# Fused attention and gated FFN on one core: gate and value sums in chunks among the first batch's scores, a new arrangement of units, stores held at block ends

## Chip, cores and metric

One Trainium2 chip, one of its cores. The metric is the device time of one execution in microseconds (us), the median of several runs. The inputs are float32 in HBM; the kernel computes in bf16 with float32 sums.

## What is computed

```python
# q, k, v: (8, 12, 448, 64); w_gate, w_val: (768, 1536); w_out: (1536, 768)
scores = (1 / sqrt(64)) * q @ k.T                 # per batch and head
attn   = maximum(scores, 0) ** 2 / 448
x      = attn @ v                                 # heads side by side: (3584, 768)
out    = (gelu(x @ w_gate) * (x @ w_val)) @ w_out # (3584, 768)
```

## The kernel before

**Tiles.** TensorE works as four 64x64 quadrants. A sum over 128 rows is cut into a lower row half (`PE0`, r = 0) and an upper one (`PE1`, r = 1), each of two column halves; lower steps of one unit run beside upper steps of another. The 448 tokens of a batch are seven chunks of 64, the twelve heads six pairs (`pr`), two pairs are one third `m` of a batch.

**Units.** For each of the 8 batches there are
- transposes `t` (q and k to `qkT`): batches 0 and 1 on TensorE (`add_transposes`, L628; products with `ident`, L646, the copy out of PSUM L650, for the very first L609 and L617), later ones by DMA transposes on SP's queue (`add_dma_transposes`, L466, issue L480) after a regrouping copy (L475);
- 21 score units `s` (`add_scores`, L677): product `sp<-qkT`, relu on ScalarE (L714, `rl`), square on VectorE (L728, `attnT`). A score unit u belongs to third u // 7; each fourth in a third serves both pairs;
- 6 value units `v` (`add_values`, L761): product `ff<-attnT,v`, scaled copy into `xT` (L792);
- gate and value sums (`add_gate_value`, L1023): per block `fc` of 128 columns of the FFN one sum over six steps `dc` (one for each pair of heads) with `wg` and one with `wv`, gelu on ScalarE (L1044), product with the value sum on VectorE (L1049) into `uT`. From batch 1 on a part of the blocks goes in seven products of a Strassen-like scheme (`add_pair`, L911);
- output products in groups of four chunks of tokens (`add_product`, L1160), seven products with sums on VectorE between them, and stores of `osb` to `out` (L1241): four per group on SP's queue; the last two groups' tiles are stored in halves on SP's and ScalarE's queues.

All TensorE products go through the helper `mm` (L365); products on `warm` (L567, L1430) are filler that keeps TensorE busy while nothing else can run.

**Order.** A planner (`run_plan`, L109) places all operations at build time by costs and due times and writes them down engine by engine; the chip then runs each engine's stream in that order. What it is told:
- `START` (L29) lists the units of batch 0 in order, 0.8 us apart on a scale that ends near 0; this part of TensorE's lower order (`PE0`) is fixed. `PLACE5 = -7.0` (L836) puts the last value unit v5, batch 1's first transposes and three lower steps each of gate 0 and value 0 at one place near its end (L1028).
- `LINE` (L12) lists all later units: a single digit is the next gate or value sum of that batch, `2A1` one of the seven products for batch 2, `a1` one of an output group. `SHIFT` (L35) sets the spans over which scores and values of batches 2 to 7 are spread.
- Loads are issued on GpSimd's queue in the order of L1267 to L1291: q, k, v of batch 0, weight chunk 0, q and k of batch 1 for heads 0 to 3, weight chunk 1, q and k for heads 4 to 7, and so on. The tiles of q and k are two in a ring, so a load waits for the transposes of the third that had its tile.
- `Blocks` (L73) counts TensorE's instructions (a weight load and a product each) in blocks of 256. Marks are set 36 instructions ahead of a block's end; a DMA transpose (`gate`, L139) is planned behind such a mark, and its issue waits for the marked product.
- Stores of groups from the ninth on (`HELD = 8`, L1105; `op.hold`, L147) that the planner would start between 110 instructions ahead of a block's end and 4 behind it are moved to that end, and wait for the product there.

Of the kernel before, what the change touches and what calls it, by code (L numbers as in the profile page):

```python
# [12 lines left out]
0 0 0 0 0 0 0 0 0 0 0 0 0 0 0 0 0 0 0 0 0 0 0 0 1 1A1 1 2 1A6 2 2 1 1A7 1A2 1A5 2 a1 2 a2 2A1 1A4 1  # L13
1 1 1A3 1 2 1 2A2 a6 1 2A7 a7 2 1 a5 1 1 2A6 2 2 1 1 1 1 a3 1 1 a4 1 1 b1 b7 c1 b2 b6 2A4 2 c6 b4 b5
c7 c5 2B1 2B6 c4 2B2 c3 b3 2A5 2 c2 2B7 2B4 2B5 2A3 2 3A1 2 3A2 2 2B3 2 2 3A6 3A7 d7 d1 3B1 d2 4C1
3B2 3 3C1 3B7 3 d6 3 e1 d4 3C7 3 3C6 3 3B6 e7 3B4 e6 3A4 3A5 3 3 3 3C2 3 3B5 3 3 d5 3C4 3A3 3C5 d3
4A1 4C2 3B3 3C3 e5 3 4A7 f1 f2 f6 e4 f7 4C7 4 e2 4C6 4A2 e3 g7 4B1 f5 4B6 4 4A6 4B2 g1 4B7 4 g2 4A5
4C5 4A4 4B4 4B5 f4 4D7 4D1 4C4 4 5B1 5 4D6 4D5 4A3 4 g6 4 g5 4C3 4B3 f3 4 5 5B2 4D2 4D4 g3 4D3 5C1
g4 5B6 5B7 5C2 5B5 5A1 4 5A6 5 5C7 5A7 5A2 5 5B4 5D1 h1 5A4 5D6 5D2 h6 5C6 h7 5 5D7 5D5 5A5 6A1 5B3
5 5C5 5C4 5A3 5C3 5D4 6B1 5 5D3 5 6A2 6B2 h4 i1 i2 6B7 6A6 i7 h5 6A7 h2 6D1 6F7 6D7 h3 j1 6D6 6C1  # L20
6D2 i6 j7 6E1 j6 6C7 6C2 6E7 i5 i4 6C6 6B6 6A5 6A4 6E6 6A3 6F1 6B4 6B5 6C5 6D5 6D4 6F6 i3 6B3 6F5
6C4 j5 6D3 6E2 6F2 6E5 6F4 6C3 6F3 6E4 6E3 7E7 j2 7E1 7B1 k1 k7 7E2 7A1 7B2 7B7 k2 7B6 7E6 j4 7C1 k6
7A2 l7 7C7 7C6 7A7 7B4 7C2 l1 7B5 7B3 k5 7A6 7F1 j3 7D1 7E5 7F7 7F2 7A5 k4 7F6 7E4 l6 7D7 7C4 7D2
7F4 7D6 7D5 7D4 7D3 l2 7F5 7A4 7C5 7C3 7E3 7A3 l5 l4 7F3 m1 n1 m7 k3 l3 m2 m6 n6 m5 n7 n4 m3 n5 n2
m4 n3
# [4 lines left out]
t00 s0 s1 t01 s2 s3 s4 s5 t10 s6 s7 v0 s8 t11 v1 s9 s10 s11 t20 s12 s13 v2 s14 t21 s15 v3 s16 s17  # L30
s18 s19 v4 s20
# [3 lines left out]
SHIFT = "-183 -79.5 40.75 1.75 -343.75 -112 43.75 -179.5 27.25 -513.5 -447.25 0.25"  # L35


class Op:


    def __init__(self, engine, cost, emit, deps=(), lag=0.0, prio=0, other=None):
# [8 lines left out]
        self.hold = False  # L50
# [22 lines left out]
class Blocks:  # L73


    def __init__(self, size, first, lead, near=(0, 0)):
# [4 lines left out]
        self.near, self.edge, self.edges = near, size, []  # L81

    def add(self, ins, n=2):
        self.count += n
        if not self.edges or self.edges[-1][1] is not None:
            if self.count + self.near[0] >= self.edge:
                self.edges.append((self.now, None, None))
        elif self.count >= self.edge + self.near[1]:
            self.edges[-1] = self.edges[-1][0], self.now, ins
            self.edge += self.size  # L90
        if self.count + self.lead >= self.next:
            self.marks.append((self.now, ins))
            self.next += self.size

# [14 lines left out]
def run_plan(queues, pools, units, banks, arrivals, together, fill, blocks, span):  # L109
# [9 lines left out]
    def ready(op):  # L119
# [38 lines left out]
    def next_unit(short):  # L158
# [35 lines left out]
        return best  # L194

# [3 lines left out]
    while left:  # L199
# [70 lines left out]
        op.emit()  # L270
        last = max(last, op.end)
        left -= 1
    return last
# [3 lines left out]
def kernel(  # L277
# [37 lines left out]
    GATE_T, BLOCK = 1.2, 7.1  # L315

    NPB = (0, 1, 2, 3, 4, 4, 6, 6)
    ROOM = 4
    RING_V, RING_T, RING_H, RING_R, RING_A, RING_O = 3, 3, 2, 2, 4, 4
# [39 lines left out]
    blocks = Blocks(256, 256 - 192 + 10, 36, (110, 4))  # L359
# [40 lines left out]
    def load_w12(i):  # L400
        cols = slice(i * WCH, (i + 1) * WCH)

        def emit(wt, src):
            return nc.gpsimd.dma_start(
                wt[:, :, :], src[:, cols].rearrange("(c p) f -> p c f", p=128))
        w12_op[i] = [load(4 * d_model * WCH, lambda wt=wt, src=src: emit(wt, src), rate=rate)
                     for (wt, src), rate in zip(((wg[i], moe_w_gate), (wv[i], moe_w_val)),
                                                (250e3 if i == 1 else 400e3, 400e3))]
# [6 lines left out]
    def load_qk(b, i, h0, h1, deps=()):  # L415
# [12 lines left out]
        for c0, c1, rate in (((0, SC, 400e3 if b else (300e3, 226e3, 420e3)[m]),) if b < EARLY  # L428
# [6 lines left out]
    def load_v(b, h0, h1, deps=()):  # L435

        m = h0 // 4
        for i in range(2):
# [7 lines left out]
            op = load(4 * (h1 - h0) * VC * P * D, emit, deps, rate=(4e6 if h0 == 0 else 400e3) if b == 1 else 400e3 if b else 300e3)  # L446
# [19 lines left out]
    def add_dma_transposes(b, m, deps=()):  # L466
# [28 lines left out]
        for op in tr_op[b, m]:  # L495
            op.gate = GATE_T
        qk_used[b, m] = [copy]
# [130 lines left out]
    def add_transposes(at, b, m, rs):  # L628
# [6 lines left out]
        def emit(r):  # L635
            if b == 0:
                t = new_bank(box["k", r], t_op[b, m, r], [128, SC, 2 * P], bf16)
            else:
                if not box:
                    box["S"] = psS[n].tile([128, 2, 1024], bf16, name="sp", tag="S")  # L640
                t = box["S"][:, r, 0:SC * 2 * P].rearrange("d (c x) -> d c x", c=SC)
            box[r] = t
            src = qk16[b, m].rearrange("p h (c d) -> p h c d", d=D)
# [10 lines left out]
        for r in rs:  # L654
# [6 lines left out]
            mine = b == 0 and f"t{m}{r}a" in START.split()  # L661
# [99 lines left out]
    def add_values(at, b, pr):  # L761
# [6 lines left out]
        def emit(i, w):  # L768
            if 0 not in box:
                box[0] = new_bank(box["k"], x_op[b, pr])  # L770
            if (i, w) == (1, VC - 1) or last and (i, w) == (0, 1):
# [42 lines left out]
        if last:  # L814
            ops[1][0].after = ops[0][1]
            for o, p in zip(ops[1], ops[1][1:]):
                p.after = o
            ops[0][2].deps.append(ops[1][3])
            for i in range(2):
                lower.append((at - 0.6, ops[0][i]))  # L820
# [676 lines left out]
```

## Time and profile before

| | us |
|---|---|
| three timed runs | 396.62, 398.0, 400.57 (median 398.0) |
| profiled execution | 396.92 |
| its span, first to last instruction | 394.9 |

The span is what the rows of the profile cover; the profiled execution's own time is 2.0 us longer. The granted TensorE clock in it is 0.998. In the rows, PE is TensorE's products, PEld its weight loads, DVE VectorE, ACT ScalarE, POOL GpSimd, SP SyncE; `ff`, `sp` are tiles in PSUM. "x72" is a count; behind the bar stand busy us and mean ns of one, then idle time of the engine ahead of the group and what ended it. "issue" is time in which an engine waited for nothing that the profile shows.

### The profile page before, as it was taken

To read this page: it belongs to the slowest core of one execution; us is meant where nothing else is said; L and a number is where in the kernel's file an instruction comes from. 1 tells how busy PE (TensorE), PEld (TensorE's weight loads), DVE (VectorE), ACT (ScalarE), POOL (GpSimd) and SP (SyncE) were. 2 spreads that over 40 slices of the span, in tenths; PEclk is the share of its full clock that TensorE was granted. 3 is DMA by queue.
4 is the path that set the end of the run, shared out by engine and by line. 5 is a ranking of instruction groups with operands and counts; after the bars stand their busy time and mean duration, and the time that the engine had idled before them with its cause. 6 is when DMAs were issued, how large, how long until landed. Compare 5 with 4: busy or idle time off the path is not lost.

```text
span 394.9 us, 22904 instructions
## 1 busy us (share of the span) xinstructions
PE 386.3 (98%) x10570; PEld 358.4 (91%) x10573; DVE 309.6 (78%) x522; ACT 258.7 (66%) x401; POOL 97.2 (25%) x156
## 2 busy tenths in 40 slices
PE   7999999999999999999999999999999999999995
PEld 3458889999999999999999999989999999999994
DVE  3885779968797499999797779758988999866772
ACT  5866872357677767787786478765787886535541
POOL 7656523322233323232332123310211000000000
PEclk9999999999999999999999999999999999999999
DMA  8999999988999969887999598880763501121134
GB/s 110 186 199 199 197 209 185 112 103 83 161 148 175 152 85 143 93 132 121 113 148 108 124 122 111 139 83 11 103 105 56 125 6 43 45 45 45 43 85 120
DMA packets 85567, 45.12 MB, mean 114 GB/s; under 512 B 46048, under 2 KB 82400, under 8 KB 85472
## 3 DMA queue, kind: packets, MB, share of 16 engines
q0 software_dynamic: 46944, 24.39, 49.9%
q1 hardware_dynamic: 37888, 18.49, 26.4%
q8 instruction: 82, 1.34, 1.4%
q10 hardware_dynamic: 640, 0.79, 0.6%
q14 instruction: 13, 0.11, 0.1%
HBM read 48.76 MB, written 11.01 MB: 151 GB/s over the span
## 4 chain that ended last, share of the span: by engine, by line
PE 93%; DVE 2%; DMA 2%; POOL 1%; issue 1%; ACT 0%; ACTq 0%; POOLq 0%
PE ff L365 85%; PE sp L365 7%; DMA qk<-in_k_dram 2%; DVE attnT L728 1%; PE sp L646 1%; POOL qk L424 1%; DVE xT L792 0%; PE ff L646 0%; ACTq L1241 0%; ACT osb L1225 0%; ACT rl L714 0%; PE ff L567 0%; DVE osb L1223 0%; DVE qkT L650 0%; POOL ident masks.py:199 0%
## 5 line engine op out<-in xcount | busy, mean ns | idle before, releaser
L714 ACT ACTIVATE rl<-sp 128x896 bf16<-128x896 f32 x168 | 152.1, 919 | 50.4 <-PE sp L365 45.1
L365 PE MATMUL ff<-xT,wg 64*64 64x224 bf16 (+1 forms) x2304 | 183.7, 299 | 0.6 <-issue 0.6
L365 PEld LDWEIGHTS <-wv 64*64 64x64 bf16 x2304 | 127.7, 107 | 4.4
L365 PEld LDWEIGHTS <-wg 64*64 64x64 bf16 x2304 | 123.3, 107 | 5.0 <-issue 0.5
L365 PE MATMUL ff<-xT,wv 64*64 64x448 bf16 x1056 | 120.8, 349 | 0.0
L728 DVE TENSOR_TENSOR attnT<-rl 128x1792 bf16<-128x1792 bf16 (+1 forms) x98 | 92.2, 952 | 6.6 <-ACT rl L714 6.2
L365 PEld LDWEIGHTS <-ws 64*64 64x64 bf16 x1872 | 92.3, 107 | 1.4 <-issue 1.0
L365 PEld LDWEIGHTS <-s 64*64 64x64 bf16 x1344 | 81.6, 107 | 1.8
L365 PE MATMUL ff<-attnT,v 64*64 64x448 bf16 (+1 forms) x768 | 79.7, 326 | 0.7 <-DVE attnT L728 0.6
L365 PE MATMUL ff<-ts,wv 64*64 64x224 bf16 x1248 | 78.7, 256 | 0.0
L365 PE MATMUL ff<-ts,ws 64*64 64x224 bf16 x1248 | 77.6, 256 | 0.0
L365 PE MATMUL sp<-qkT 64*64 64x448 bf16 (+1 forms) x768 | 74.6, 328 | 0.7 <-issue 0.3
L365 PE MATMUL ff<-wo,s 64*64 64x384 bf16 x672 | 63.4, 323 | 0.0
L966 DVE TENSOR_TENSOR part<-ff,part 128x448 f32<-128x448 f32 x78 | 47.5, 622 | 20.1 <-PE ff L365 16.4
L365 PEld LDWEIGHTS <-uT 64*64 64x64 bf16 x1008 | 62.5, 107 | 0.7
L365 PE MATMUL ff<-wt,s 64*64 64x384 bf16 x672 | 61.4, 322 | 0.0
L365 PE MATMUL ff<-wo,uT 64*64 64x384 bf16 x672 | 60.7, 322 | 0.0
L962 ACT COPY part<-ff 128x448 f32<-128x448 f32 x78 | 41.3, 534 | 12.4 <-PE ff L365 11.2
L443 POOL DMA_DIRECT2D v<-in_v_dram x48 | 29.6, 620 | 80.3 <-ACT rl L714 44.3
L365 PEld LDWEIGHTS <-v 64*64 64x64 bf16 x768 | 44.7, 107 | 4.1 <-issue 1.7
L424 POOL DMA_DIRECT2D qk<-in_q_dram x43 | 27.6, 642 | 80.0 <-ACT rl L714 59.5
L1049 DVE TENSOR_TENSOR uT<-gel,ff 128x448 bf16<-128x448 bf16 x44 | 27.3, 620 | 22.4 <-PE ff L365 11.0
(51 smaller groups left out, 423.9 us busy)
## 6 DMA issues: line engine op xcount, KB each, us to landing
out_dram<-osb SPq DMA_DIRECT2D x48, 192.0 KB, 3.3
v<-in_v_dram POOLq DMA_DIRECT2D x48, 128.0 KB, 4.1
wg<-in_moe_w_gate_dram POOLq DMA_DIRECT2D x6, 384.0 KB, 10.4
wv<-in_moe_w_val_dram POOLq DMA_DIRECT2D x6, 384.0 KB, 11.0
wo<-in_moe_w_out_dram POOLq DMA_DIRECT2D x4, 576.0 KB, 14.9
qk<-in_q_dram POOLq DMA_DIRECT2D x18, 128.0 KB, 3.5
qk<-in_k_dram POOLq DMA_DIRECT2D x18, 128.0 KB, 4.3
qk<-in_q_dram POOLq DMA_DIRECT2D x18, 96.0 KB, 3.8
```

What stands on the lines that cost most here:

```text
L365: ins = nc.tensor.matmul(o, lhsT, rhs, start=start, stop=stop, skip_group_check=onto, tile_position=(P * row, P * col))
L424: return nc.gpsimd.dma_start(qk16[b, m][HALF[i], r0:r0 + h1 - h0, cols], src[b, h0:h1].rearrange("h (p c) d -> p h (c d)", c=SC)[:, :, cols])
L443: return nc.gpsimd.dma_start(v16[b, m][HALF[i], h0 % 4:h0 % 4 + h1 - h0, :, :], v[b, h0:h1].rearrange("h (p c) d -> p h c d", c=SC)[:, :, ...
L646: blocks.add(nc.tensor.transpose(t[HALF[j], c, :], src[:, 2 * r + j, c, :], ident[:, :], tile_position=(0, P * j)))
L714: relu.ins = nc.scalar.activation(duo["rl"][:, u % 2, :, :], box[0][:, :, 0:S], AF.Relu).ins
L728: nc.vector.tensor_tensor(a[:, part], duo["rl"][:, part], duo["rl"][:, part], op=ALU.mult)
L962: rd.ins = nc.scalar.copy(st["t", name][:, :], box[0][:, 0:S]).ins
L966: rd.ins = nc.vector.tensor_tensor(t[:, :], box[0][:, 0:S], t[:, :], op=ALU.add).ins
L1049: u_op[b, fc].ins = nc.vector.tensor_tensor(uT[b][:, fc, :], gel.pop((b, fc))[:, :], box[0][:, 0:S], op=ALU.mult).ins
```

## The change

Five things change.
1. `START` can name `g0`, `g1`, `h0` (steps of gate 0, value 0 and gate 1), `T` (batch 1's first transposes), `w` (the first three lower steps of v5), and `S0`, `S1` (batch 1's first scores). Five lower steps of gate 0 and five of value 0 stand among the last score units; the sixth of each follows at the end. For gate 1 the upper half goes first (`turned`), from the place of `h0` on. `t11` and `t20` stand earlier among the scores. v4's copy goes to ScalarE (`v4a`), and so does the copy of the first of batch 1's transposes (`T_ACT`).
2. `LINE` and `SHIFT` hold another arrangement.
3. Both halves of a third's transposes of batch 1 are written in one run.
4. On SP's and GpSimd's queues, instructions are written down through a queue of their own (`held`). A store of any group but the last, which would be written within 110 instructions ahead of a block's end, is written, with all behind it on its queue, when 4 instructions are left, and waits for the product written last. The rule by planned time and `HELD` go.
5. The order of loads: weight chunk 1 behind batch 1's q and k of heads 4 to 7, v of heads 4 to 7 behind weight chunk 3. The planner's rates of loads are others.

```diff
 START = """
-t00 s0 s1 t01 s2 s3 s4 s5 t10 s6 s7 v0 s8 t11 v1 s9 s10 s11 t20 s12 s13 v2 s14 t21 s15 v3 s16 s17
-s18 s19 v4 s20
+t00 s0 s1 t01 s2 s3 s4 s5 t10 s6 t11 s7 v0 s8 v1 s9 s10 t20 s11 s12 s13 v2 s14 t21 s15 s16 g0 v3 g0
+s17 g0 s18 s19 v4a s20 g1 g0 g1 T w g1 g1 v5 h0 S0 S1 g1 g0
 """
-SHIFT = "-183 -79.5 40.75 1.75 -343.75 -112 43.75 -179.5 27.25 -513.5 -447.25 0.25"
+SHIFT = "-162 -50.25 25.5 2.75 -445.25 -51.75 31.25 -216.75 14.5 -671.5 -361 -10.5"
...
 class Blocks:
...
+    def ahead(self, near, before):
+        edge = -(-(before + near[1]) // self.size) * self.size
+        return edge - near[0] <= before and self.count < edge - near[1]
...
 def run_plan(...):
...
-        if op.hold:
-            for begin, end, ins in blocks.edges[-3:]:
-                if t >= begin and (end is None or t < end):
-                    if end is None and not forced:
-                        return None
-                    t, op.mark = end or t, ins
-            return t
...
+    held = {"SP": deque(), "POOL": deque()}
+    def release(whole=False):
+        for waiting in held.values():
+            while waiting:
+                op, count = waiting[0]
+                if not whole and op.near and blocks.ahead(op.near, count):
+                    break
+                waiting.popleft()
+                if op.near and blocks.count > count:
+                    op.mark = blocks.last
+                op.emit()
+                if waiting:
+                    waiting[0] = waiting[0][0], blocks.count
...
-        op.emit()
+        if e in held:
+            held[e].append((op, blocks.count))
+        else:
+            op.emit()
+        release()
...
+    NEAR_STORE, NEAR_QK, NEAR_V, NEAR_T = (110, 4), None, None, None
...
             else:
-                if not box:
-                    box["S"] = psS[n].tile([128, 2, 1024], bf16, name="sp", tag="S")
-                t = box["S"][:, r, 0:SC * 2 * P].rearrange("d (c x) -> d c x", c=SC)
+                if box:
+                    return
+                box["S"] = psS[n].tile([128, 2, 1024], bf16, name="sp", tag="S")
+                for i in rs:
+                    box[i] = box["S"][:, i, 0:SC * 2 * P].rearrange("d (c x) -> d c x", c=SC)
+                    transpose(i)
+                return
...
-            mine = b == 0 and f"t{m}{r}a" in START.split()
+            mine = f"t{m}{r}a" in START.split() if b == 0 else m == 0 and r < T_ACT
...
 def add_gate_value(at, b, fc, g):
-        if (b, fc) == (0, 0):
-            at = [PLACE5 - 0.5 + 0.1 * g] * 3 + [0.01 * g] * 3
+        early = chunks0.get(f"{'gh'[fc]}{g}") if b == 0 and fc < 2 else None
+        turned = bool(early) and fc == 1
+        if early:
+            at = (early + [0.1 * fc + 0.01 * g] * KC)[:KC]
...
+        if turned:
+            ops[0][0].deps.append(ops[1][-1])
+            for n, op in enumerate(ops[1]):
+                if n:
+                    op.after = ops[1][n - 1]
+                op.prio = 1
+                pairs.append(("from", early[0], [op]))
+            for n, op in enumerate(ops[0]):
+                lower.append((0.1 * fc + 0.01 * g, op))
+        else:
+            then(at, GS, *ops, box, lambda: done)
...
-            op.hold = gr >= HELD
+            op.near = NEAR_STORE if gr < B * SC // 4 - 1 else None
...
     load_qk(1, 0, 0, 4)
     load_qk(1, 1, 0, 4)
-    load_w12(1)
     load_qk(1, 0, 4, 8)
     load_qk(1, 1, 4, 8)
+    load_w12(1)
     load_v(1, 0, 4)
     load_w12(2)
-    load_v(1, 4, 8)
     load_qk(1, 0, 8, 12)
     load_qk(1, 1, 8, 12)
     load_w12(3)
+    load_v(1, 4, 8)
     load_v(1, 8, 12)
```

More of the change, by code (lines that the diff above doesn't have):

```diff
@@ L1 @@
 import math
+from collections import deque
 from contextlib import ExitStack
@@ L18 @@
[L18 to L22, printed above, removed]
@@ L49, in __init__ @@
         self.gate = 0.0
-        self.hold = False
+        self.near = None
         self.mark = None
@@ L73, with __init__ @@
 class Blocks:
-    def __init__(self, size, first, lead, near=(0, 0)):
+    def __init__(self, size, first, lead):
         self.size, self.lead = size, lead
@@ L496, in add_dma_transposes @@
             op.gate = GATE_T
+            op.near = NEAR_T
         qk_used[b, m] = [copy]
@@ L770, in emit @@
                 box[0] = new_bank(box["k"], x_op[b, pr])
-            if (i, w) == (1, VC - 1) or last and (i, w) == (0, 1):
+            if (i, w) == (1, VC - 1) or last and (i, w) == (0, 2):
                 wait_lower(box)
@@ L814, in add_values @@
         if last:
-            ops[1][0].after = ops[0][1]
+            ops[1][0].after = ops[0][2]
             for o, p in zip(ops[1], ops[1][1:]):
                 p.after = o
-            ops[0][2].deps.append(ops[1][3])
-            for i in range(2):
-                lower.append((at - 0.6, ops[0][i]))
-                lower.append((at, ops[0][i + 2]))
+            ops[0][3].deps.append(ops[1][3])
+            for i in range(4):
+                lower.append((placed0["w"] if i < 3 else at, ops[0][i]))
             for hi in ops[1]:
-                pairs.append(("with", ops[0][1], hi))
+                pairs.append(("with", ops[0][2], hi))
         else:
@@ L835 @@
     G, R = KC * GS, FC // 2 * RS
-    PLACE5 = -7.0
-    placed0 = {x.rstrip("a"): -60.0 + 0.8 * n for n, x in enumerate(START.split())}
+    placed0, chunks0 = {}, {}
+    for n, x in enumerate(START.split()):
+        placed0[x.rstrip("a")] = -60.0 + 0.8 * n
+        if x[0] in "gh":
+            chunks0.setdefault(x, []).append(-60.0 + 0.8 * n)
     ws, ws_op, ts, ts_op, ts_used = {}, {}, {}, {}, {}
@@ L1038, in emit @@
                 ins = mm(box[0][HALF[j], 0:S], w[HALF[r], dc, o + P * j:o + P * (j + 1)],
-                         xT[b][HALF[r], dc, :], r, j, r == 0 and dc == 0, r == 1 and dc == KC - 1)
+                         xT[b][HALF[r], dc, :], r, j, not second and dc == 0, second and dc == KC - 1)
             box[1] = ins
@@ L1407 @@
             upper.append((tau[place[lo]], hi))
+        elif kind == "from":
+            upper.append((tau[sum(at < lo for at, _ in lower)], hi[0]))
         else:
@@ L1445 @@
                 op.behind.append(relus[(*thirds[n - 2], PACE[4 + i])])
-        for op in (*qk_loads[b, m], *v_loads[b, m]):
-            op.deps += op.behind
+        for near, ops in ((NEAR_QK, qk_loads[b, m]), (NEAR_V, v_loads[b, m])):
+            for op in ops:
+                op.deps += op.behind
+                op.near = near if b >= EARLY else None
     for new, old in zip(duos[RING_A:], duos):
```

76 lines of the change are left out of this document (41 added, 35 removed).

## The prediction

> **What bounds the kernel now.** I read the page first, then TensorE's waits, then the start alone, because the page says where time can still be found. Its lines:
>
> ```profile
> span 394.9 us, 22904 instructions
> PE 386.3 (98%) x10570; PEld 358.4 (91%) x10573; DVE 309.6 (78%) x522; ACT 258.7 (66%) x401; POOL 97.2 (25%) x156
> ```
>
> TensorE is covered for 98% of the span. Cover is not work, though: filler products count as busy, and so does a stretch in which only one half of the rows computes. TensorE's waits after 34 us (weight loads in the second line) are two lines:
>
> ```profile
> PE ff L365 <- issue: 0.6, 1, 0.6
> PEld L365 <- issue: 1.5, 4, 0.8
> ```
>
> So from 34 us on TensorE waits for almost nothing, and 361 of 395 us hold at most some 1.5 us to win. The start is different. These are TensorE's groups in the window from 4.8 to 29 us, shapes kept apart; behind the bar stand the busy us and the mean ns:
>
> ```profile
> L365 PE MATMUL sp<-qkT 64*64 64x448 bf16 x72 | 7.8, 363 | 0.4 <-ACT qkT L617 0.2
> L365 PE MATMUL ff<-attnT,v 64*64 64x448 bf16 x72 | 7.4, 350 | 0.7 <-DVE attnT L728 0.6
> L567 PE MATMUL ff<-warm 128*128 128x512 bf16 x10 | 3.4, 384 | 0.2 <-issue 0.2
> L365 PE MATMUL ff<-attnT,v 64*64 64x224 bf16 x24 | 3.1, 262 | 0.1
> L646 PE MATMUL ff<-ident,qk 128*64 128x128 bf16 x70 | 2.9, 222 | 0.7 <-DMA qk<-in_k_dram 0.6
> L365 PE MATMUL ff<-xT,wg 64*64 64x448 bf16 x10 | 1.3, 359 | 0.0
> L365 PE MATMUL sp<-qkT 64*64 64x224 bf16 x24 | 1.2, 267 | 0.3 <-issue 0.3
> L646 PE MATMUL sp<-ident,qk 128*64 128x128 bf16 x28 | 1.0, 221 | 0.0
> L365 PE MATMUL ff<-xT,wv 64*64 64x448 bf16 x6 | 0.7, 349 | 0.0
> L609 PE MATMUL ff<-ident,qk 128*64 128x128 bf16 x14 | 0.6, 220 | 0.4 <-DMA qk<-in_k_dram 0.4
> ```
>
> How fast TensorE goes when nothing holds it is read from the distance of like rows in a full stretch (timeline): 0.19 us a step for 448 columns, so half of that for 224, and a run of 14 transposes takes 0.51 us (chain).
>
> ```profile
> 249.72 0.38 PE L365 MATMUL ff<-xT,wv 64*64 64x448 bf16 x2
> 249.91 0.38 PE L365 MATMUL ff<-xT,wv 64*64 64x448 bf16 x2
> 31.95 0.51 PE sp L646 x14
> ```
>
> A step of both row halves is four 64x64 products. The window then holds (72+72+10+6)/4 x 0.19 = 7.6 us, (24+24)/4 x 0.095 = 1.1 us and (70+28+14)/14 x 0.51 = 4.1 us: 12.8 us of work in 24.2 us. Some 11 us of TensorE are empty or filler there, and the first change works on this stretch. What sets the order in that stretch is the chain of work that ended last, here for 10 to 34 us:
>
> ```profile
> 18.15 0.62 DVE xT L792
> 18.77 2.14 DVE attnT L728 x4
> 20.91 0.54 DVE qkT L650
> ...
> 24.65 0.54 DVE attnT L728
> ```
>
> For 7 us, 18.15 to 25.19, VectorE alone is the chain, and ScalarE runs beside it (timelines, idle time in brackets; the last row is VectorE's, the last copy to xT of batch 0):
>
> ```profile
> 15.46 2.54 ACT L714 ACTIVATE rl<-sp 128x896 bf16<-128x896 f32 x3 [0.58 <-PE sp L365]
> 18.33 7.52 ACT L714 ACTIVATE rl<-sp 128x896 bf16<-128x896 f32 x9 [0.34 <-PE sp L365]
> 30.30 1.73 ACT L714 ACTIVATE rl<-sp 128x896 bf16<-128x896 f32 x2 [4.45 <-PE sp L365]
> 27.94 0.62 DVE L792 TENSOR_SCALAR xT<-ff 128x448 bf16<-128x448 f32 x1 [0.19 <-PE ff L365]
> ```
>
> Nine relus take 7.52 us, 0.84 each, so the 21 of batch 0 cannot take under 17.6 us however TensorE is filled. Gate and value sums can end only behind the last copy to xT, at 28.56, but steps whose pairs are there can start before it. After 25.85 us ScalarE idles for 4.45 us until batch 1's first scores.
>
> **Part by part.**
>
> *Chunks of gate and value sums.* Before, three lower steps each of gate 0 and value 0 stand early. After, START holds five of each, and `h0` brings six upper steps of gate 1: 16 for 6. Ten more at half an array are 10 x 0.19 / 2 = 0.95 us of full TensorE moved from behind 28.56 us into the holes. They need weights; the gate's issue on GpSimd and its us to landing are:
>
> ```profile
> 11.94 0.84 POOL L404 DMA_DIRECT2D wg<-in_moe_w_gate_dram  x1
> wg<-in_moe_w_gate_dram POOLq DMA_DIRECT2D x1, 384.0 KB, 7.4
> ```
>
> It has landed at 19.3 us, and the value's load is the next in the queue. The first `g0` stands behind s16, whose relu is the fifth of the nine, so near 21 us; the first `g1` stands behind s20, near 24. Cover of about 2 us. If it were gone, TensorE would stand at the chunk, and the scores written behind it with it. Bounds: 0 (they only push scores back) to 0.95. I take **0.8**, near the upper end, since the holes are far larger than the work.
>
> *t11 before s7, t20 before s11.* In the old order t11 and v1 stand together before s9:
>
> ```profile
> 13.85 0.58 PE L646 MATMUL ff<-ident,qk 128*64 128x128 bf16 x14
> 14.36 0.86 PE L365 MATMUL ff<-attnT,v 64*64 64x448 bf16 x16
> ```
>
> They fill TensorE from 13.85 to 15.2 us, and s9 comes behind them; that is the 0.58 us for which ScalarE waits before 15.46 (quoted above); t11's data is there already, as t10 uses the same loads. Moved, t11 takes the place of filler. t20 moved ahead of s11 can cost one run, 0.51, or save the 0.34. VectorE's copies do not grow. Bounds -0.5 to 0.9; I take **0.6**, as ScalarE's 0.58 is the firmest of them.
>
> *Batch 1's first transposes and two scores earlier; one copy of them and v4's copy on ScalarE.* Two score units are 2 x 0.19 = 0.4 us of TensorE moved into holes. The transposes' copy (0.54 on VectorE, on ScalarE at most a relu's 0.84) and v4's lie in the 4.45 us; without that cover each delays a relu by its own length. Bounds -0.8 to 1.0; **0.4**.
>
> *Transposes in one run.* Only (1,1) was split in two. TensorE's weight loads waited 0.9 us in three such places between 25 and 34 us:
>
> ```profile
> PEld L646 <- issue: 0.9, 3, 0.4
> ```
>
> One place fewer is 0.3. **0.2**; bounds 0 to 0.4.
>
> *Loads.* Batch 1's second q and k go ahead of weight chunk 1 on GpSimd's queue, and they wait for t21:
>
> ```profile
> 20.64 0.64 POOL L424 DMA_DIRECT2D qk<-in_q_dram  x1 [3.01 <-PE ff L646]
> 21.27 0.64 POOL L424 DMA_DIRECT2D qk<-in_k_dram  x1
> qk<-in_k_dram POOLq DMA_DIRECT2D x1, 224.0 KB, 10.1
> ```
>
> Chunk 1's two loads are then issued at 21.9 us at the earliest. Before, this k was the last of the four to land, at 31.4; the bytes are the same, so chunk 1 is now the last, at about 31.4. It is needed after gate and value 0 and 1, four sums of 6 x 0.19 = 1.14 us less the 16 half steps (1.5), so some 3 us behind 27.8 when nothing lies between. Cover about zero; transposes of 0.51 each and scores of 0.19 lie between. Queued behind it on GpSimd are v(1,0) and chunk 2, whose products come later still. If the cover is gone, the gate of block 2 waits, at most for the two loads put ahead, which are 448 KB against 768 of the chunk: some 2.4 us by the landing of 10.1. Bounds -2.4 to 0; **0**.
>
> *Stores held at block ends.* The wait to be avoided shows once, with no engine as its releaser:
>
> ```profile
> 266.12 0.25 PE L365 MATMUL ff<-xT,wg 64*64 64x224 bf16 x1 [0.65 <-issue]
> q8 instruction: 82, 1.34, 1.4%
> q8 instruction: 1, 0.02, 1.7%
> ```
>
> The second row is the page's instruction queue, the third the same in 262 to 267 us. One block there took 1.7% of 16 x 5 us = 1.4 us, against 1.4% of 16 x 394.9 us / 82 = 1.1 on the mean. A late instruction block fits it. But in these 5 us SP issued a transpose and no store, so the hold would not have helped here. Upper bound the 1.5 us of waits; lower bound the third rival's -8; I take **0.4**, near the waits and well under them. The Trainium skill (Runtime: NRT & Kernel Launch, section Instruction fetch mechanics) says that the next 16 KiB block is fetched while the current one runs and that the crossing is "mostly hidden". By that rule this term is 0 and the sum is 0.4 us smaller; the wait of 0.65 us is against it as an always, the other blocks, 82 with 4 waits on weight loads, are for it.
>
> *Another LINE and SHIFT.* The same products in another order. As nothing waits after 34 us, a gain is at most the 1.5 us already counted; a loss has no bound in the trace; I put six waits like the longest one at 265 us (0.65) as its end, -4. **0**.
>
> *At nothing.* The planner's load rates move no instruction by themselves. The last pair of values has three lower steps ahead instead of two; a step is 0.19, so the bounds are -0.2 and 0.2, under the cover of VectorE's chain.
>
> **The sum.** 0.8 + 0.6 + 0.4 + 0.2 + 0.4 = 2.4 us. The profiled execution took 396.92 us over its span of 394.9; 394.5 follows. The three timed runs are 396.62, 398.0 and 400.57, so their median lies 1.1 above the profiled one. With all of that kept the median would be 395.6; I let half of it go, as the hold is the one part that could make executions more alike: the forecast for the median is **395.0 us**.
>
> **The rivals.**
>
> *The start fills up (392.0 us).* Chance 0.26. The holes hold 11 us, and VectorE's chain could end 0.9 us sooner with the rest packed tightly: 4 us at the start (of 11), 0.9 of the 1.5 us of waits, and the whole 1.1 of the median: 398.0 - 6.0 = 392.0. For it: ScalarE's 4.45 us. Against it: 17.6 us of relus stay.
>
> *The gain is only a shift (398.0 us).* Chance 0.12. The chunks take the holes, but chunk 1 of the weights comes 2.4 us later, and gate 2 waits for what the start saved: 2.4 - 2.4 = 0. For it: the queue order above; against it: transposes and scores that can go in between.
>
> *The stores hold up the transposes (403 us).* Chance 0.20, slower. SP's queue carries both:
>
> ```profile
> out_dram<-osb SPq DMA_DIRECT2D x48, 192.0 KB, 3.3
> qkT<-qkr SPq DMA_TRANSPOSE x36, 4.6
> 200.00:250.00 50.00, 50.00 (x1447) 49.08 (x1442) 40.68 (x70) 35.89 (x57) 12.29 (x20) 1.00 0.86 119
> ```
>
> A held store waits for TensorE, and everything behind it on SP waits too. The window is 106 of 256 instructions, 53 products, at 50 us / 1447 = 35 ns at most 1.8 us, and catches 4 stores in 10: of the 32 of groups 0 to 7 some 13. If six of them push back a transpose that a score needs at once, TensorE, whose stream is one written order, stands 6 x 1.2 (two thirds of the longest hold) = 7 us, and 395.0 + 7, with another 1 for the stores themselves in the queue, is about 403. It decides from the point where a transpose lands behind its score. Against it: at present no score waits for a transpose at all, so there is some slack; and the landing time of 4.6 us is longer than a hold. The new LINE could do the same at other places, so I do not set it low.
>
> **Chances.** Forecast 0.42, rivals 0.26, 0.12, 0.20. One percent, 4 us, is about what a measurement of this kernel can tell from no change. Faster than 394.0: the second case and 0.12 of the forecast, **0.38**. Within: 0.30 of the forecast and the shift, **0.42**. Slower than 402: **0.20**. The range is 391.0 to 402.0; the forecast's own is 392.5 to 397.5.
>
> **What would show it.** Right: the last copy to xT of batch 0 ends about 27.8 instead of 28.56 us; batch 1's first relu starts before 28.5 instead of 30.30; the 448-column steps on wg and wv before 29 us grow from 16 products to over 30; after 34 us TensorE's waits stay under 2 us. Wrong: score products that wait for a qkT from SP, a wait on wg or wv between 29 and 34 us, or holes in windows after 60 us.

## The result: 1.2% slower, and where the profile after puts it

The changed kernel takes 401.81 us (median of 6 runs, 401.15 to 404.48) where the kernel before takes 397.35 beside it: ratio 1.0118, interval 1.0083 to 1.0152. A second time, on another chip, it was 401.8 against 397.87, ratio 1.0101 (1.0075 to 1.0127). The profiled execution took 401.62 us; the head of its page and its instruction queue:

```profile
span 399.8 us, 22908 instructions
PE 388.7 (97%) x10571; PEld 351.7 (88%) x10571; DVE 309.3 (77%) x520; ACT 261.0 (65%) x403; POOL 96.3 (24%) x156
q8 instruction: 82, 1.34, 1.4%
```

The span is 4.9 us longer, and the work is the same. Where the time went is read from the busy time by windows. First after, then before; the columns are busy us and instructions of PE, PEld, DVE, ACT and POOL, then the granted clock, the DMA share and GB/s:

```profile
4.80:29.00 24.20, 23.39 (x361) 13.65 (x362) 18.31 (x33) 20.15 (x25) 15.81 (x25) 1.00 1.28 178
29.00:34.00 5.00, 5.00 (x113) 3.19 (x107) 2.40 (x5) 3.32 (x6) 2.65 (x4) 1.00 1.45 197
34.00:64.00 30.00, 29.16 (x631) 23.45 (x624) 21.05 (x31) 19.60 (x27) 11.84 (x17) 1.00 1.33 203
64.00:400.00 336.00, 327.56 (x9474) 310.12 (x9464) 267.30 (x453) 216.39 (x346) 62.31 (x101) 1.00 0.69 100
```

```profile
4.80:29.00 24.20, 21.89 (x338) 12.04 (x343) 18.81 (x34) 18.21 (x22) 14.99 (x23) 1.00 1.32 186
29.00:34.00 5.00, 5.00 (x104) 3.50 (x103) 2.72 (x4) 2.10 (x3) 3.49 (x5) 1.00 1.44 197
34.00:64.00 30.00, 30.00 (x656) 26.11 (x652) 21.73 (x31) 20.92 (x30) 11.91 (x17) 1.00 1.33 202
64.00:400.00 336.00, 326.08 (x9476) 315.52 (x9466) 266.09 (x453) 215.98 (x346) 63.14 (x101) 0.99 0.68 99
```

Count the products. From the span's start to 34 us the changed kernel does 27 more (481 against 454; the first two windows leave out the first 4.8 us, and what runs across 29 us stands in both). From 34 to 64 us it does 25 fewer, and behind 64 us both have the same left: 9474 and 9476 (317.8 and 317.9 us of a full array, when each product is weighted by its tile and columns). Those take 399.8 - 64 = 335.8 us after, 394.9 - 64 = 330.9 before. So the lead of the start is gone by 64 us, and the loss of 4.9 us lies wholly behind it. The waits of TensorE's weight loads that the profile calls issue, for the whole span, 34 to 64 us, and from 64 us on, show the same. After:

```profile
PEld L380 <- issue: 13.0, 29, 1.1
PEld L380 <- issue: 2.0, 3, 1.1
PEld L380 <- issue: 6.5, 11, 1.1
```

Before:

```profile
PEld L365 <- issue: 5.9, 16, 0.8
PEld L365 <- issue: 0.5, 2, 0.3
PEld L365 <- issue: 1.0, 2, 0.8
```

6.5 - 1.0 = 5.5 us more waiting behind 64 us, for 4.9 us of span. Nothing in the kernel is the releaser of these waits: no tile is late. One of them, at 138 us, seen close, with TensorE's products and the weight loads from 134.15 to 139.40:

```profile
138.23 0.38 PE L380 MATMUL ff<-ts,wv 64*64 64x224 bf16 x4
139.48 0.28 PE L380 MATMUL ff<-attnT,v 64*64 64x224 bf16 x2 [0.87 <-issue]
134.15:139.40 5.25, 4.07 (x130) 1.00 1.05 97
```

The instruction queue's 82 packets carry 1.34 MB for TensorE's 21,142 products and weight loads: 16 KB and some 256 instructions each, so 128 weight loads and 128 products. Counted along the stream, 13 of the 14 waits from 34 us on stand where such a block begins (the other, 0.16 us at 124.8, does not), and so do all four of the kernel before. One is here, and the block before it began 128 weight loads earlier, near 134.1. The DMA queues from 134.2 to 136.8 us (first two rows, no packet of the instruction queue), and the instruction queue from 136.8 to 138.3:

```profile
q0 software_dynamic: 524, 0.26, 116.1%
q1 hardware_dynamic: 365, 0.09, 42.6%
...
q8 instruction: 1, 0.02, 5.7%
```

For 2.6 us behind the crossing only loads, transposes and stores move. Then the one block comes; it took 5.7% of 16 x 1.5 us = 1.4 us, so it is there near 138.2, and TensorE goes on at 139.4 to 139.5, 1.25 us later. The reading: at each crossing TensorE asks for the next block, the fetch gets its turn behind transfers already in flight, and when delay, transfer and some 1.3 us together exceed the time that TensorE needs for one block, it stands (here 2.7 + 1.4 + 1.3 = 5.4 us against 4.1). Counted in the same way over the blocks between 72 and 312 us (packet's start less the crossing, by the loads, transposes and stores that landed later) of before, after and the first four experiments below, the fetch began in the median 0.7 us behind the crossing with no transfer in flight (31 blocks), 1.3 with four (64) and 3.5 with eight (three only). The scatter is wide, 0.1 to 2.7 us with four, so the number of transfers does not fix the delay. Over 2 us late were one of 52 blocks before and five of 51 after.

A late fetch also takes back the start's lead, between 34 and 64 us. With the weights arriving, the DMA is full, and the fetch comes late for both kernels. After, the crossing at 39.6 us has its block only in the second of two windows, 39.6 to 44.1 and 44.1 to 45.4:

```profile
q0 software_dynamic: 1786, 0.88, 144.7%
...
q8 instruction: 1, 0.02, 4.7%
```

Before, the crossing came at 40.7 us, and its block began to move at 44.17, after at 44.19: here the fetch keeps the time of the transfers, not TensorE's. Whoever arrives earlier only waits longer (1.1 us at 45.4, in the 2.0 above). The block that the fetch brings begins at 46.54 after and at 46.49 before: a lead of 1.2 us at one crossing is gone at the next.

The start itself did part of what was forecast. Products from 4.8 to 29 us, and of ScalarE and VectorE the first relus of batch 1 and the last copy to xT of batch 0:

```profile
L380 PE MATMUL sp<-qkT 64*64 64x448 bf16 x80 | 9.4, 362 | 0.3 <-ACT qkT L632 0.2
L380 PE MATMUL ff<-xT,wg 64*64 64x448 bf16 x18 | 2.5, 350 | 0.0
L380 PE MATMUL ff<-xT,wv 64*64 64x448 bf16 x10 | 1.7, 354 | 0.0
28.68 1.73 ACT L737 ACTIVATE rl<-sp 128x896 bf16<-128x896 f32 x2 [0.88 <-PE sp L380]
28.49 0.62 DVE L815 TENSOR_SCALAR xT<-ff 128x448 bf16<-128x448 f32 x1 [0.48 <-PE ff L380]
```

28 products on wg and wv for 16, eight more of scores: 20 x 0.19 / 4 = 0.95 us of work more in the same time. In a second profile of either kernel (below) it is 11 products, 0.5 us.

### The profile page after: what moved, and what is told of

Same layout as the page of the kernel before. It is cut to its first block, busy times and chain, and to the rows that moved or that the text cites. A ratio compares the mean times of both kernels' runs of the same rounds, so it can differ in the third digit from the quotient of the medians.

```text
span 399.8 us, 22908 instructions
## 1 busy us (share of the span) xinstructions
PE 388.7 (97%) x10571; PEld 351.7 (88%) x10571; DVE 309.3 (77%) x520; ACT 261.0 (65%) x403; POOL 96.3 (24%) x156
## 3 DMA queue, kind: packets, MB, share of 16 engines
q8 instruction: 82, 1.34, 1.4%
## 4 chain that ended last, share of the span: by engine, by line
PE 94%; DVE 2%; issue 1%; ACT 1%; ACTq 0%; DVEq 0%
PE ff L380 83%; PE sp L380 8%; DVE attnT L751 1%; PE ff L1473 1%; ACT rl L737 1%; PE sp L669 1%; PE ff L669 1%; PE ff L582 0%; DVE qkT L673 0%; DVE xT L815 0%; ACTq L1280 0%; PE ff L624 0%; ACT osb L1264 0%; DVE part L991 0%; DVE osb L1262 0%
## 5 line engine op out<-in xcount | busy, mean ns | idle before, releaser
L380 PE MATMUL ff<-xT,wg 64*64 64x224 bf16 (+1 forms) x2304 | 179.9, 299 | 1.4 <-issue 1.4
L380 PEld LDWEIGHTS <-wg 64*64 64x64 bf16 x2304 | 119.7, 107 | 8.2 <-issue 2.6
L380 PEld LDWEIGHTS <-wv 64*64 64x64 bf16 x2304 | 121.9, 107 | 5.6 <-issue 0.4
L380 PE MATMUL ff<-attnT,v 64*64 64x448 bf16 (+1 forms) x768 | 84.4, 326 | 1.1 <-issue 0.9
L380 PEld LDWEIGHTS <-s 64*64 64x64 bf16 x1344 | 77.6, 107 | 3.4 <-issue 1.0
L380 PE MATMUL sp<-qkT 64*64 64x448 bf16 (+1 forms) x768 | 78.1, 328 | 0.4 <-ACT qkT L632 0.2
L380 PE MATMUL ff<-ts,wv 64*64 64x224 bf16 x1248 | 75.6, 256 | 0.0
L380 PE MATMUL ff<-wo,uT 64*64 64x384 bf16 x672 | 62.6, 323 | 0.0
L380 PE MATMUL ff<-wt,s 64*64 64x384 bf16 x672 | 59.5, 323 | 0.0
L987 ACT COPY part<-ff 128x448 f32<-128x448 f32 x78 | 40.7, 534 | 12.6 <-PE ff L380 11.7
L1264 ACT COPY osb<-ff 128x384 f32<-128x384 f32 x56 | 26.8, 480 | 30.7 <-PE ff L380 30.5
L457 POOL DMA_DIRECT2D v<-in_v_dram x48 | 29.5, 621 | 68.9 <-ACT rl L737 44.8
```

The lines of the kernel that those rows point to most:

```text
L380: ins = nc.tensor.matmul(o, lhsT, rhs, start=start, stop=stop, skip_group_check=onto, tile_position=(P * row, P * col))
L457: return nc.gpsimd.dma_start(v16[b, m][HALF[i], h0 % 4:h0 % 4 + h1 - h0, :, :], v[b, h0:h1].rearrange("h (p c) d -> p h c d", c=SC)[:, :, ...
L987: rd.ins = nc.scalar.copy(st["t", name][:, :], box[0][:, 0:S]).ins
L1264: ins = nc.scalar.copy(o, box[0][:, 0:OGS])
```

## The experiments

Theory A: the new arrangement (LINE, SHIFT, order and rates of loads) puts TensorE's block crossings where transfers are in flight, and this is the loss. Rivals: the held stores, the chunks, or a slower order of the sums by itself.

**Stores not held, in the kernel after.**

```diff
-    NEAR_STORE, NEAR_QK, NEAR_V, NEAR_T = (110, 4), None, None, None
+    NEAR_STORE, NEAR_QK, NEAR_V, NEAR_T = None, None, None, None
```

> The kernel after, with no store held at block ends; everything else as after. Theory A (the new LINE and SHIFT put loads and DMA transposes where TensorE's instruction blocks are fetched, and the blocks come late): the holds do not matter, 401 to 403 us, and waits of weight loads on nothing of about 13 us as after. Theory B (a store let go at the block's end starts together with the fetch of the next block and delays it): the waits fall to about 6 us, as before, and the time to 396.5 to 398.

Ratio to before 1.0075 (1.0029 to 1.0121), span 399.2 us, waits for issue behind 64 us 5.4 us in 12 places. With the hold it was 1.0118 and 1.0101 on other chips, and the intervals overlap. The ten runs spread from 401.05 to 410.93 us, and the ratio of the plain medians, 405.07 and 400.7, is 1.0109. The hold is not the loss; whether it adds some 0.3% stays open.

**The new arrangement alone, in the kernel before:** LINE, SHIFT, order and rates of loads as in after.

```diff
-SHIFT = "-183 -79.5 40.75 1.75 -343.75 -112 43.75 -179.5 27.25 -513.5 -447.25 0.25"
+SHIFT = "-162 -50.25 25.5 2.75 -445.25 -51.75 31.25 -216.75 14.5 -671.5 -361 -10.5"
-    load_w12(1)
     load_qk(1, 0, 4, 8)
     load_qk(1, 1, 4, 8)
+    load_w12(1)
...
```

> The kernel before with LINE, SHIFT, the order of loads and the planner's load rates of after; START, the holds by planned time from group 8 on and the split transposes stay. Theory A (arrangement): 401 to 403 us, with 5 to 8 us of waits of weight loads on nothing after 60 us. Theory B (holds): 396.5 to 398.5 us, with under 2 us of such waits after 60 us.

Ratio 1.0128 (1.0079 to 1.0177). Its waits from 64 us on, more than the 5 to 8 us expected:

```profile
PEld L365 <- issue: 9.6, 18, 1.5
```

The loss comes without chunks, without the new holds and without the run of transposes. That part of Theory A is shown; what LINE and SHIFT do in it and what the order and rates of loads do is not separated.

**The kernel after without the chunks** (START as before, with T and w at its end).

```diff
-t00 s0 s1 t01 s2 s3 s4 s5 t10 s6 t11 s7 v0 s8 v1 s9 s10 t20 s11 s12 s13 v2 s14 t21 s15 s16 g0 v3 g0
-s17 g0 s18 s19 v4a s20 g1 g0 g1 T w g1 g1 v5 h0 S0 S1 g1 g0
+t00 s0 s1 t01 s2 s3 s4 s5 t10 s6 s7 v0 s8 t11 v1 s9 s10 s11 t20 s12 s13 v2 s14 t21 s15 v3 s16 s17
+s18 s19 v4 s20 w v5 T
```

> The kernel after with batch 0 in the order of before: no chunks of gate and value sums, t11 and t20 and v4's copy where they were, the last values and batch 1's transposes at the end. Theory Q (from about 45 us on TensorE runs as fast as instruction blocks arrive, whose times the loads set): TensorE is 0.8 to 1.5 us later at 34 us but not at 58 us, and the time is within 1 us of after. Rival (the start's gain reaches the end, and other things cost more): 402.8 to 403.5 us, and the lag of 34 us is still there at 300 us.

Ratio 1.0116 (1.0072 to 1.0159), span 403.5 us, 10.8 us of waits in 22 places behind 64 us. Without the chunks the loss is as large. At 34 us this kernel is 37 products behind the kernel after (444 for 481), behind 64 us both have nearly the same left (9480 and 9474): the start's lead is worth nothing in the end. Its last copy to xT of batch 0 ends at 28.44 us:

```profile
27.82 0.62 DVE L815 TENSOR_SCALAR xT<-ff 128x448 bf16<-128x448 f32 x1 [0.48 <-PE ff L380]
```

**At most four early loads in flight, in the kernel after:** each load from the first weights to w_out waits for the load four ahead of it.

```diff
+            if back and n >= 14:
+                tc.add_manual_dep(ins.ins, loads[n - back].ins.name, SYNC, reason="depth")
```

> The kernel after, in which each early load from weight chunk 0 up to w_out waits until the load four places ahead of it has landed; the plan and all orders are the same. Theory Q (between 30 and 64 us a block of instructions waits behind all loads that are already queued): fetches start under 2 us behind the crossing instead of 3.5 to 5, the waits at 45, 52, 58 and 69 us go, and the time falls by 2 to 3 us to about 399.5. Rival (the fetch only gets its share of busy DMA engines, however deep the queue): fetches start 3.5 to 5 us behind the crossing as now, and the time stays at 401 to 403 or grows, as loads start later.

Ratio 1.0254 (1.0211 to 1.0298). The first fetches came sooner (27.6 to 29.5 us, and 34.1 to 34.9), but the one asked for at 40.1 still only at 45.5, and behind 64 us the waits grew to 11.7 us. That the number of early loads queued is the whole delay falls. The loads now come more slowly, 172 GB/s from 34 to 64 us for 203; that they therefore end later and meet later blocks is likely, not shown.

**The kernel after again, and before again: a second profile of each.**

> The kernel after, unchanged, for comparison on the same chip as the next three. 1.008 to 1.015 of before; waits of weight loads on nothing after 64 us of 5 to 8 us.

> The kernel before, unchanged, one profile on the same chip. Waits of weight loads on nothing after 64 us of 1 to 3 us.

After again: waits behind 64 us 6.6 us in 13 places, span 400.3. Before again: 2.6 us in 4 places, span 396.9. In this pair 4.0 us more waiting stand for 3.4 us of span. Two executions of one kernel differ by up to 1.6 us in this sum, the two kernels by 3.9 to 5.6.

**Fewer loads.** Theory L: loads in flight delay the fetch. The loads of v from batch 1 on and of q and k from batch 2 on are left out and older tiles are read in their place, so the output is not the reference's; first in the kernel after, later in the kernel before.

```diff
         def emit(c0, c1):
+            if b >= 2:
+                qk16[b, m] = qk16[1, 1 + (b + m) % 2]
+                return None
...
             def emit(i=i):
+                if b >= 1:
+                    v16[b, m] = v16[0, m]
+                    return None
                 if (b, m) not in v16:
```

> The kernel after without the loads of v from batch 1 on and of q and k from batch 2 on (older tiles are read in their place); all products, transposes and stores stay, in the same order. Theory L (what delays the fetch of a block of instructions is the loads in flight when it is asked for): after 72 us the fetches start 0.3 to 1 us behind the crossing, the waits of weight loads there fall under 1 us, and the start's lead over before is kept beyond 58 us; 389 to 393 us on a chip where before takes 397, a ratio of 0.98 to 0.99. Theory T (DMA transposes or stores delay them): the waits after 72 us stay at 4 us or more and the ratio is 1.00 to 1.01.

> The kernel before, leaving out the same loads as few_loads (v from batch 1 on, q and k from batch 2 on, so its output is not the reference's). It separates what the two arrangements cost by themselves from what they cost through the loads. Theory L (the late instruction blocks, delayed by loads in flight, are the whole difference behind 64 us): both arrangements then run without stalls there, so this one ends within 1 us of few_loads (ratio to before 0.990 to 0.996), and loses 1 to 2 us against before. Rival (the new arrangement is slower by itself, through order of sums or copies): without loads the old arrangement stays 3 us or more ahead of few_loads, ratio about 0.985.

Ratios to before 0.9928 (0.9901 to 0.9955) and 0.9948 (0.9929 to 0.9967): 395.67 and 395.48 us. Waits from 64 us on, the kernel after's first:

```profile
PEld L380 <- issue: 0.7, 3, 0.4
```

```profile
PEld L365 <- issue: 0.2, 1, 0.2
```

This settles two things. Without the loads the waits are gone, and with them the late fetches (none of 53 blocks over 2 us late in either kernel), so the loads cause them. And the two arrangements then take the same time, as far as the intervals tell: the new order of sums is not slower by itself. The kernel after stays above the 389 to 393 us expected. The lead of the start doesn't show here either, since the weights are still loaded: the kernel after without these loads keeps 1.7 us of waits between 34 and 64 us, the kernel before 0.2.

**Loads and stores held until 60 instructions behind a crossing, in the kernel after.**

```diff
-    NEAR_STORE, NEAR_QK, NEAR_V, NEAR_T = (110, 4), None, None, None
+    NEAR_STORE, NEAR_QK, NEAR_V, NEAR_T = (110, -60), (110, -60), (110, -60), None
```

> The kernel after, in which q, k, v loads of batch 2 on and stores that would be written from 110 instructions ahead of a block's end to 60 behind it are all held to 60 behind it. Theory L: fewer transfers are in flight at the crossings, the waits of weight loads after 64 us fall by half or more, and the ratio to before comes to 0.995 to 1.005. Rival (the loads come too late for their scores, or the same transfers collide with the next crossing): waits move to other places and the ratio stays at 1.01 or grows.

Ratio 1.0218 (1.0169 to 1.0267); waits behind 64 us 9.6 us in 15 places, the longest now 2.7. The fetches of 12 of 50 blocks now begin over 2 us behind their crossing, with three to six transfers in flight: held, the transfers bunch up and meet the next fetch. The remedy fails.

**Moving the crossings.** Theory P: the old order's time is that of one good alignment of crossings and transfers. Each of the 16 warm-up products at the very start is cut into three, five or seven over the same columns: 64, 128 or 192 instructions more ahead of the first data. The written order is otherwise the same on all engines; the crossings lie a quarter, a half or three quarters of a block earlier in the work.

```diff
-                blocks.add(nc.tensor.matmul(t[HALF[j], :], warm[:, HALF[j]], warm[:, :],
-                                            start=True, stop=True, tile_position=(0, P * j)))
+                lo = 0
+                for n in (256, 64, 64, 64, 64):
+                    ins = nc.tensor.matmul(t[HALF[j], lo:lo + n], warm[:, HALF[j]], warm[:, lo:lo + n],
+                                           start=True, stop=True, tile_position=(0, P * j))
+                    lo += n
+                blocks.add(ins)
```

> The kernel before with 64 instructions more ahead of the first data (each warm-up product cut into three), crossings a quarter of a block earlier in the work. Theory P (the old order's 398 us are those of one good alignment; at others it loses as much as the new one): 401 to 405 us on a chip where before has 398, weight loads waiting for issue 9 us or more. Rival P2 (half a block is the one bad alignment, since there the DMA transposes, planned to be issued just ahead of a crossing, are in flight at the crossing): within 2 us of before.

> The kernel before, with each of the 16 warm-up products cut into five over the same columns: 128 instructions more on TensorE ahead of the first data, nothing else moved on any engine. Every crossing of a block of instructions is then half a block earlier in the work. Theory P (the old order is good only because its crossings lie where few transfers are in flight, an accident of alignment): it comes out 3 to 6 us slower, with weight loads waiting for issue 8 us or more in all, against 5.9. Rival (the old arrangement leaves fewer collisions wherever the crossings lie): within 1.5 us of before, waits of 5 to 7 us.

> The kernel before with 192 instructions more ahead of the first data (each warm-up product cut into seven), the last of the four quarter shifts. Theory P: 401 to 405 us on a chip where before has 398, waits for issue 9 us or more. Rival P2: within 2 us of before.

> The kernel after, with each of the 16 warm-up products cut into three: 64 instructions more ahead of the first data, crossings a quarter of a block earlier in the work, nothing else moved. Theory P: the stalls move to other crossings and their sum changes by more than 2 us one way or the other (against 13.0 for weight loads), with the time following by about the same. Rival (the new arrangement collides at any phase): waits 12 to 14 us, time within 1 us of after (ratio 1.008 to 1.013).

> The kernel after, with each of the 16 warm-up products cut into five: 128 instructions more, crossings half a block earlier in the work. Theory P: as at 64, a sum of waits that differs by more than 2 us from 13.0, and from that at 64; the best of the phases may come near before (ratio 1.000). Rival: waits 12 to 14 us and ratio 1.008 to 1.013 again.

> The kernel after with 192 instructions more ahead of the first data. With 0, 64 and 128 it had ratios of 1.010 to 1.012, 1.014 and 1.017. Theory P: the new arrangement has a good alignment too, and if it is this one, the ratio is 0.995 to 1.003, with the start's 1.2 us kept as far as 34 us; otherwise 1.010 to 1.018, and then no quarter shift frees the new arrangement. Rival (the new arrangement collides at any alignment): 1.010 to 1.018.

Ratio to the kernel before (its interval), and the waits for issue behind 64 us:

| instructions more | before's order | waits | after's order | waits |
|---|---|---|---|---|
| 0 | 1 | 1.0 | 1.0118 (1.0083 to 1.0152) | 6.5 |
| 64 | 1.0074 (1.0038 to 1.0110) | 3.3 | 1.0138 (1.0093 to 1.0182) | 8.4 |
| 128 | 1.0164 (1.0127 to 1.0200) | 9.8 | 1.0171 (1.0138 to 1.0203) | 8.6 |
| 192 | 1.0057 (1.0023 to 1.0090) | 3.3 | 1.0176 (1.0141 to 1.0210) | 11.2 |

Before's order with 128, and after's with 192, from 64 us on:

```profile
PEld L365 <- issue: 9.8, 18, 1.4
```

```profile
PEld L380 <- issue: 11.2, 17, 2.4
```

With the written order kept and the crossings half a block earlier, the old kernel lost 6.5 us: more than the change under study did. So the old kernel's "nothing waits after 34 us" belongs to its alignment. The smaller pieces also take time of their own: the first transposes start at 5.28 us with 128 instructions more and at 5.57 with 192, for 4.88 and 4.97 in the two profiles of before. That is no account of the 6.5 us (with 128 the last copy to xT of batch 0 ends at 28.39, no later than the 28.56 and 28.39 of before). With 64 and 192 it ends at 29.17 and 29.19, so of their 2.9 and 2.3 us up to 0.8 can be this. Theory P as written, that every other alignment costs 3 us or more, is shown for the half block alone; the quarters, 2.9 and 2.3 us by their ratios with intervals from 0.9 to 4.4, lie between P and P2. On the mean of the four the old order stands at 1.0074, the new one at 1.0151. So of the 1.18% as built, 0.77 is the difference of the means, the new order colliding at each of the four; the other 0.41 comes from the old order standing 0.74 below its own mean, the new one only 0.33. None of the four frees the new order. For it Theory P expected the whole sum of waits, 13.0 us, to move by more than 2: it is 12.8, 13.3 and 15.6, so with 64 and 128 that did not come. One thing goes along with the shift and isn't separated from it: the DMA transposes wait for products picked ahead of the planned crossings, and keep to those products. And four points don't say what lies between them.

**t11 alone moved ahead of s7, in the kernel before.**

```diff
-t00 s0 s1 t01 s2 s3 s4 s5 t10 s6 s7 v0 s8 t11 v1 s9 s10 s11 t20 s12 s13 v2 s14 t21 s15 v3 s16 s17
+t00 s0 s1 t01 s2 s3 s4 s5 t10 s6 t11 s7 v0 s8 v1 s9 s10 s11 t20 s12 s13 v2 s14 t21 s15 v3 s16 s17
```

> The kernel before with t11 alone moved ahead of s7 in START, as after has it; LINE, SHIFT, loads and holds stay. The prediction's step gave 0.6 us for this and t20 together. As a step by itself: ScalarE's wait of 0.58 us ahead of 15.46 goes, the last copy to xT of batch 0 ends 0.4 to 0.7 us earlier, and the span falls by as much (ratio 0.998 to 1.000). Theory P: the planner places what follows a little otherwise and two instructions fewer stand ahead, so crossings meet other transfers, and that alone is worth -1 to +5 us: the start's gain shows at 34 us and is not to be found in the time (ratio 1.000 to 1.012).

Ratio 1.0049 (1.0023 to 1.0076), slower. Its ScalarE, the last copy to xT of batch 0, and the waits from 64 us on:

```profile
13.20 4.24 ACT L714 ACTIVATE rl<-sp 128x896 bf16<-128x896 f32 x5 [0.23 <-PE sp L365]
17.99 7.52 ACT L714 ACTIVATE rl<-sp 128x896 bf16<-128x896 f32 x9 [0.55 <-PE sp L365]
27.58 0.62 DVE L792 TENSOR_SCALAR xT<-ff 128x448 bf16<-128x448 f32 x1 [0.18 <-PE ff L365]
PEld L365 <- issue: 5.9, 14, 0.9
```

The wait of 0.58 us ahead of 15.46 is gone, as the step said, but 0.55 instead of 0.34 now stand ahead of the nine relus. They begin 0.34 us earlier, and the last copy ends at 28.20 instead of 28.56. This is at the edge of what can be told: with the old START the copy ends at 28.39 in the second profile and at 28.20 in the kernel before with few loads. The planner then places what follows a little otherwise, and behind 64 us 4.9 us more are waited (3.3 against the second profile). A gain of at most some 0.4 us became a loss of about 2.

None of these kernels computes the whole result faster than the kernel before.

## Why the prediction was wrong, step by step

- **The step that failed: "Another LINE and SHIFT: 0", and "as nothing waits after 34 us".** The arrangement alone, with its order and rates of loads, measures 1.0128, some 5 us, and the waits behind 64 us went from 1.0 us to 6.5. The absence of waits was read as slack. It held for one placing of the crossings: with these half a block earlier, the same written order waits 9.8 us. The bound of -4 us, six waits of 0.65, had the right mechanism and place, but was given no weight beside a value of 0. Nine waits more came behind 64 us (11 for 2), 0.6 us each. The prediction's own sign of being wrong, holes after 60 us, is what came.
- **"A late instruction block fits it"** was right for the row at 266 us, and should have been carried to all 82 blocks: how far each was from being late was there to be read, from the instruction queue's packets by windows.
- **The rule "mostly hidden"** (Trainium skill, Runtime: NRT & Kernel Launch, section Instruction fetch mechanics): most of the 82 crossings of either kernel are indeed hidden. The 13 of the kernel after from 34 us on that wait, where there had been four, are not, and they are the result. The prediction took the rule's side where it counted: it judged the blocks by how many had waited.
- **Chunks, 0.8 us; scores and copies, 0.4; t11 and t20, 0.6; one run, 0.2: 2.0 us at the start.** At 29 us 0.95 us was there, 0.5 in the second profiles. The chunks and scores moved as said (28 products on wg and wv, not over 30; the first relu of batch 1 at 28.68, not before 28.5, and 30.30 before). But the last copy to xT ended at 29.11, not at 27.8: 0.55 later than before, not 0.76 earlier (29.48 and 28.39 in the second profiles). t11 by itself is worth at most some 0.4 there. With the old START in the changed kernel the copy ends at 28.44 (its row stands with that run), so the new START as a whole holds it up by some 0.7; that this is what it writes between the last scores and values is likely, not separated. No chunk waited for its weights (0.0 in their rows from 4.8 to 29 us).
- **That a lead at the start reaches the end** was assumed in all terms. The lead was taken back between 34 and 64 us, by a fetch that keeps the time of the DMA. The second rival, "only a shift", had this outcome for the start, with another cause: weight chunk 1 was not waited for. Nor does the 2.4 us put on the two loads ahead of it follow from the landing of 10.1 us that it names; 448 KB at the 186 to 197 GB/s of the windows are 2.3 to 2.5 us.
- **Stores held, 0.4 us:** no gain shows; the kernel without the hold is not shown to be slower (1.0075 and 1.0118, the intervals overlap).
- **The third rival, 403 us,** names nearly the time, and not the reason: no score waited for a transpose, in the profile after or without the hold.
- **The range** of 391 to 402 holds the 401.8 at its edge. Its upper end is before's 398 and the one per cent allowed for the measurement, and no case of the prediction stood for a loss of 4 us by late blocks: that the time lies inside is luck.

## What to carry to other kernels

A TensorE stream without waits is not a stream with slack: before an order is changed, read from the instruction queue's packets how late each block is, against the time that one block of work takes. Where the DMA is full, an earlier start only meets the same late fetch. When two arrangements differ by a per cent or so, shift the instruction count ahead of each and compare over several alignments, or the better place is taken for the better order.

## What the hardware showed that was not expected

- The fetch of an instruction block waits behind data transfers: in the median 0.7 us behind the crossing with none in flight, 1.3 with four, 3.5 in the three blocks with eight, and 2.8 to 4.6 us while the weights arrive (the crossings from 27 to 64 us of the kernel after). TensorE goes on 1.26 to 1.61 us after the packet's end, in all twelve waits of over 0.3 us at a crossing of the kernel after.
- 128 instructions of filler more ahead of the first data, which start the first transposes only 0.3 to 0.4 us later, make a kernel of 398 us 1.6% slower.
- Leaving out all loads of q, k and v behind the first batches makes the kernel before only 0.5% faster (395.48 us) and the kernel after 1.5% (395.67 for 401.80), though it takes the DMA share behind 64 us from 0.69 to 0.32: the loads are no bound, but collide.
